# Sixteen subtractions of layer 1's weights move from the vector engine to GpSimd

## The chip, the cores and the metric

The kernel runs on one core of a Trainium2 chip. The metric is the device time of one execution in microseconds (us), as a median over runs. The core has a matrix engine (PE, also TensorE), a vector engine (DVE), a scalar engine (ACT), GpSimd (POOL) and a queue engine that issues transfers (SP). Each engine works through its own instructions strictly in the order in which the program put them, and waits on semaphores where an instruction needs another engine's result.

## The reference

The work is an attention block with a memory term, followed by two feed-forward layers; all results are float32.

```python
scores = scale * np.matmul(q, k.transpose(0, 1, 3, 2))      # B, H, S, D = 4, 8, 576, 64
...
a = np.exp(scores)
a /= a.sum(-1, keepdims=True) + 1e-09
local = np.matmul(a, v)
...
return (g * mem_out + (1 - g) * local).astype(np.float32)

h = x @ w_in                                                # 2304 x 512 by 512 x 2048
r = np.maximum(h, 0.0)
g = s * (r * r) + b
return (g @ w_out).astype(np.float32)                       # 2304 x 2048 by 2048 x 512
```

The second layer has the same two products with a leaky relu between them. The weights `w_in` and `w_out` of both layers arrive as 64-bit floats.

## The kernel before, in words

Attention is done batch by batch (b = 0 to 3) and in each batch for four pairs of heads; each pair is done in two sets of query chunks, so that a batch has eight output groups. One group goes through every engine in turn: scores on PE (L758), row maxima on DVE (L731), exponentials on ACT (L724), the sums' reciprocals on DVE (L784, L786), scaling of the weights on ACT or DVE (L543, L545), transposes on PE (L558), copies of the transposes on ACT or DVE (L566, L568), and the outputs on PE (L647, L663). L647 stands at the head of each group's outputs, so its groups count how far attention is.

The feed-forward layers work on blocks of tokens. Block 0 of layer 1 has the first 512 tokens, which are ready when batch 0 of attention is done. For each of 16 slices f of the hidden width, PE does the first product in four steps of three matmuls (L906, L907, L908 into `hb`) and the second product in four steps of three (L947, L948, L949 into `yb`). Such a step of three matmuls is called a step below. Three matmuls are needed because every float32 operand is split into a high part, rounded to the PE's faster float32 format, and a low part, which is the rest: high by high, high by low, low by high.

Block 0 also prepares layer 1's weights, slice by slice, first `w_in` (x = 0, key `wi`) and then `w_out` (x = 1, key `wo`). A 512 KB piece is loaded; DVE puts a float32 together out of the two 32-bit words in three instructions (L845, L848, L851); ACT rounds it to the high part (L854); DVE subtracts the high part from the float32 and so writes the low part (L857). All are 128 partitions by 512 columns. The float32 sits in one of a few shared buffers (`room`, `pool`, `poolx`) that is free again after the subtraction. Layer 2's weights go the same way much later.

Nothing of the order is written by hand. All operations are handed to a planner with an engine and an assumed duration each. It goes through time, gives every engine the ready operation of highest rank, hands out the shared buffers as they come free, and the instructions are then put out in that order. Attention of batches 0 and 1 ranks ahead of the weights, these ahead of batches 2 and 3, and these ahead of the feed-forward matmuls, which therefore fill what attention leaves of PE. A duration that is changed for one operation can change the order of all engines behind it.

Of the kernel before, what the change touches and what calls it, by code (L numbers as in the profile page):

```python
# [78 lines left out]
class Plan:  # L79
# [17 lines left out]
    def op(self, eng, dur, fn, r=(), w=(), prio=None, bytes_=0, claim=()):  # L97
        i = len(self.ops)
        deps, late = set(), set()
        for k in r:  # L100
            if k in self.writer:
                deps.add(self.writer[k])
            self.readers.setdefault(k, []).append(i)
        for k in w:
            if k in self.writer:
                deps.add(self.writer[k])
            late.update(self.readers.get(k, ()))
            self.writer[k] = i
            self.readers[k] = []
        late -= deps  # L110
        late.discard(i)
        deps.discard(i)
        slots = []
        for k in list(r) + list(w):
            s = k[0] if isinstance(k, tuple) else k
            if isinstance(s, Slot) and s not in slots:
                slots.append(s)
                s.left += 1
        self.ops.append((eng, dur, fn, deps | late, i + self.lean if prio is None else prio, bytes_, slots, late, claim))
        return i  # L120
# [181 lines left out]
def t_dve(n, rate=1.04, extra=0.0):  # L302
    return 69 + n * rate + extra


def t_act(n, fixed=93.0, extra=0.0):
    return fixed + n * 0.834 + extra


def build(tc, kp, vd, qp, mzd, beta8, sb2, win1, wout1, win2, wout2, alpha, outT):  # L310
    nc = tc.nc
    win1, wout1, win2, wout2 = (w.bitcast(I32) for w in (win1, wout1, win2, wout2))
    V, A, T = nc.vector, nc.scalar, nc.tensor
    plan = Plan(NSLOT, 3 * XF)
    plan.edge = NSLOT - XS
    op = plan.op
    ATT, MOE, LATE = 0, 10 ** 7, 400

    with tc.tile_pool(name="sb", bufs=1) as sb, tc.tile_pool(
# [9 lines left out]
        def wt(f, x, lo):  # L329
            if f not in made:  # L330
                made[f] = sb.tile([128, 4, DM], F32R, name=f"wt{f}", tag=f"wt{f}")
            return made[f][:, 2 * x + lo, :]
# [43 lines left out]
        def at(s, n, dt=F32):  # L376

            if s.place < NSLOT:
                t, j = (pool, s.place) if s.place < NSLOT - XS else (poolx, s.place - NSLOT + XS)
                v = t[:, j * GW:(j + s.size) * GW]  # L380
            else:
                f, j = divmod(s.place - NSLOT, 3)
                v = room[KF - XF + f][:, j * GW:(j + s.size) * GW]
            return (v if dt == F32 else v.bitcast(dt))[:, 0:n]
# [50 lines left out]
        def either(kind, a_dur, a_fn, d_dur, d_fn, **kw):  # L435

            ways = {"ACT": (a_dur, a_fn)}
            if kind in FLEX:
                ways["DVE"] = (d_dur, d_fn)
            plan.either(ways, **kw)  # L440
# [375 lines left out]
        def weights(win, wout, f, layer):  # L816
            prio = None
            if layer == 1:
                prio = marks[int(WP)] + (WP - int(WP)) * (marks[1] - marks[0])
            claim = []  # L820
            if layer == 1 and f >= KF - XF:
                claim = [NSLOT + 3 * (f - KF + XF) + j for j in range(3)]
            above = max(0, 3 * (f + 1 - KF + XF))
            for src, x, key in ((win, 0, "wi"), (wout, 1, "wo")):
                sw = Slot(RES["wb" if layer == 1 else "wb2"], layer == 1, above=above)

                def whole(sw=sw, dt=F32):
                    return at(sw, 512, dt)

                st = Slot(RES["st" if layer == 1 else "st2"], layer == 1, 2, above)  # L830

                def word(x, st=st):
                    return at(st, 1024, I32).rearrange("p (n t) -> p n t", t=2)[:, :, x]

                gate = []

                first = layer == 2 and f == x == 0
                if layer == 2:
                    gate = [("x1", B - 1, NP - 1)] if first else ["claimed"]
                elif W1GATE:  # L840
                    gate = [("x1", 0, min(NP - 1, f // W1GATE))]
                op("SP", 475, lambda st=st, src=src: nc.sync.dma_start(
                    out=at(st, 1024, I32), in_=src[f]), r=gate, w=[st] + (["claimed"] if first else []), prio=prio, bytes_=524288,
                   claim=list(range(NSLOT - XS, NSLOT)) if first else [])
                op("DVE", t_dve(512, 0.52), lambda word=word, whole=whole: V.tensor_scalar(  # L845
                    out=whole(dt=I32), in0=word(1), scalar1=3, scalar2=0x3FFFFFF8, op0=ALU.logical_shift_left,
                    op1=ALU.bitwise_and), r=[st], w=[sw], prio=prio)
                op("DVE", t_dve(512), lambda word=word, whole=whole: V.scalar_tensor_tensor(  # L848
                    out=whole(dt=I32), in0=word(0), scalar=29, in1=whole(dt=I32), op0=ALU.logical_shift_right,
                    op1=ALU.bitwise_or), r=[st], w=[sw], prio=prio)  # L850
                op("DVE", t_dve(512), lambda word=word, whole=whole: V.scalar_tensor_tensor(  # L851
                    out=whole(dt=I32), in0=word(1), scalar=-0x40000000, in1=whole(dt=I32), op0=ALU.bitwise_and,
                    op1=ALU.bitwise_or), r=[st], w=[sw], prio=prio)
                either("w", t_act(512), lambda whole=whole, x=x: A.copy(out=wt(f, x, 0), in_=whole()),  # L854
                       t_dve(512, 0.52), lambda whole=whole, x=x: V.tensor_copy(out=wt(f, x, 0), in_=whole()),
                       r=[sw], w=[(key, "h", f)], prio=prio, claim=claim)
                op("DVE", t_dve(512), lambda whole=whole, x=x: V.tensor_tensor(  # L857
                    out=wt(f, x, 1), in0=whole(), in1=wt(f, x, 0).bitcast(F32), op=ALU.subtract),
                   r=[sw, (key, "h", f)], w=[(key, "l", f)], prio=prio)

# [169 lines left out]
        def moe(layer, blk, xs):  # L1030
            t0, n = BLOCKS[layer][blk]
            if (layer, blk) != (1, 0):
                load_x(layer, blk, t0, n, xs)
            for f in range(KF):
                if layer == 1 and blk == 0:
                    weights(win1, wout1, f, 1)
                if f == 0 and (layer, blk) == (1, 1):
                    flush()
                    op("ACT", 400, ones, r=["one", ("g2", KF - 1)],
                       w=["gr"] + [(x, j) for x in ("gt", "gh", "gl") for j in range(2)])  # L1040

                if layer == 1 and n == NBIG and pend[0] is not None:
                    flush()
                gj = g1(layer, n, xs, f)
                if pend[0] is not None:
                    flush()
                pend[0] = (layer, blk, f, gj)

        def flush():
            layer, blk, f, gj = pend[0]  # L1050
            pend[0] = None
            t0, n = BLOCKS[layer][blk]
            g2(layer, blk, n, f, gj)
            if layer == 1 and blk == len(BLOCKS[1]) - 1:
                weights(win2, wout2, f, 2)
            if f == KF - 1:
                evac(layer, blk, t0, n)
# [68 lines left out]
```

## Time and profile before

| | before |
|---|---|
| median of 3 runs | 1002.53 us (1000.65 to 1002.85) |
| the profiled execution's own time | 1002.58 us |
| its span in the profile | 1000.6 us |
| PE busy | 988.0 us (99%) |
| DVE busy | 584.4 us (58%) |
| ACT busy | 461.5 us (46%) |
| POOL busy | 5.1 us (1%) |

The span runs from the first to the last instruction; 2 us of the execution's own time lie around it. The busy shares are averages over a program with very different stretches, so a share says little about any one of them.

### The profile page before, as it was taken

How to read it: one execution, taken by the hardware profiler on the slowest of the kernel's cores; microseconds unless marked ns; L12 is line 12 of the kernel's file. 1: busy time of each engine (PE TensorE's matmuls, PEld its weight loads, DVE VectorE, ACT ScalarE, POOL GpSimd, SP SyncE). 2: the span in 40 equal slices, each digit the busy share in tenths (PEclk: the TensorE clock that was granted, in tenths of full speed). 3: DMA queues.
4: the chain of work that ended last, by engine and by line, in shares of the span. 5: the costliest groups of instructions: out<-in, count | busy, mean ns of one | idle time of the engine just before them, and what ended most of it. 6: DMA issues, size and time to landing. Idle time of an engine off the chain costs nothing.

```text
span 1000.6 us, 17782 instructions
## 1 busy us (share of the span) xinstructions
PE 988.0 (99%) x7032; PEld 846.0 (85%) x7032; DVE 584.4 (58%) x1422; ACT 461.5 (46%) x1160; POOL 5.1 (1%) x29
## 2 busy tenths in 40 slices
PE   7999999999999999999999999999999999999998
PEld 5677777888899888899999998888888888888898
DVE  7999998465555765534121999945334433533354
ACT  7867776576666876654454753312111111210111
POOL 1000000000000000000000000000000000000000
PEclk9999999999999999999999999999999999999999
DMA  4446434134455545444000665502000200100010
GB/s 160 150 146 230 158 129 146 45 91 107 110 124 105 139 91 103 104 119 141 1 22 1 199 187 162 158 1 85 0 1 1 74 1 1 42 1 1 1 43 22
DMA packets 86146, 85.07 MB, mean 85 GB/s; under 512 B 56880, under 2 KB 65072, under 8 KB 86064
## 3 DMA queue, kind: packets, MB, share of 16 engines
q1 hardware_dynamic: 86064, 83.95, 29.7%
q8 instruction: 55, 0.90, 0.4%
q14 instruction: 27, 0.22, 0.1%
HBM read 57.72 MB, written 13.11 MB: 71 GB/s over the span
## 4 chain that ended last, share of the span: by engine, by line
PE 93%; DVE 3%; ACT 2%; issue 1%; DMA 0%; SPq 0%; DVEq 0%; ACTq 0%
PE yb L947 14%; PE yb L949 14%; PE yb L948 13%; PE hb L906 9%; PE hb L908 8%; PE hb L907 8%; PE sp L908 3%; PE sp L907 3%; PE sp L906 3%; PE sp L758 2%; PE ob L907 2%; PE ob L906 2%; PE ob L908 2%; PE sp L663 2%; PE ob L758 1%; PE yb L758 1%
## 5 line engine op out<-in xcount | busy, mean ns | idle before, releaser
L947 PE MATMUL yb<-gr,wt 128*128 128x256 f32 (+2 forms) x832 | 273.5, 329 | 0.1
L949 PE MATMUL yb<-gr,wt 128*128 128x256 f32 (+2 forms) x832 | 271.4, 326 | 0.6 <-DVE gr L929 0.6
L948 PE MATMUL yb<-gr,wt 128*128 128x256 f32 (+2 forms) x832 | 270.0, 324 | 0.0
L906 PE MATMUL hb<-xr,wt 128*128 128x256 f32 (+1 forms) x592 | 184.7, 312 | 0.5 <-ACT gt L920 0.5
L929 DVE TENSOR_TENSOR gr<-gt,gr 128x256 fp32r<-128x256 f32 (+1 forms) x168 | 84.0, 500 | 169.9 <-ACT gr L928 169.7
L908 PE MATMUL hb<-xr,wt 128*128 128x256 f32 (+1 forms) x592 | 180.0, 304 | 0.0
L907 PE MATMUL hb<-xr,wt 128*128 128x256 f32 (+1 forms) x592 | 179.9, 304 | 0.0
L947 PEld LDWEIGHTS yb<-gr,wt 128*128 128x128 f32 x832 | 157.0, 189 | 16.7 <-issue 1.5
L949 PEld LDWEIGHTS yb<-gr,wt 128*128 128x128 f32 x832 | 156.8, 188 | 15.8 <-DVE gr L929 1.5
L948 PEld LDWEIGHTS yb<-gr,wt 128*128 128x128 f32 x832 | 156.9, 189 | 13.5
L928 ACT CAST gr<-gt 128x256 fp32r<-128x256 f32 (+1 forms) x168 | 78.6, 468 | 148.3 <-DVE gt L926 139.5
L906 PEld LDWEIGHTS hb<-xr,wt 128*128 128x128 f32 x592 | 111.7, 189 | 12.7 <-issue 5.5
L908 PEld LDWEIGHTS hb<-xr,wt 128*128 128x128 f32 x592 | 111.6, 189 | 5.7
L907 PEld LDWEIGHTS hb<-xr,wt 128*128 128x128 f32 x592 | 111.8, 189 | 4.5
L920 ACT ACTIVATE gt<-hb 128x256 f32<-128x256 f32 (+1 forms) x128 | 52.5, 410 | 118.9 <-PE hb L908 117.9
L928 ACT CAST gr<-mz 128x512 fp32r<-128x512 f32 (+1 forms) x40 | 23.1, 578 | 158.2 <-DVE mz L926 158.1
L908 PE MATMUL sp<-xr,wt 128*128 128x512 f32 (+1 forms) x160 | 59.4, 371 | 0.0
L907 PE MATMUL sp<-xr,wt 128*128 128x512 f32 (+1 forms) x160 | 59.3, 371 | 0.0
L906 PE MATMUL sp<-xr,wt 128*128 128x512 f32 (+1 forms) x160 | 59.2, 370 | 0.0
L921 ACT ACTIVATE gt<-gt 128x256 f32<-128x256 f32 (+1 forms) x128 | 57.0, 446 | 2.7
L929 DVE TENSOR_TENSOR gr<-mz,gr 128x512 fp32r<-128x512 f32 (+1 forms) x40 | 25.5, 638 | 25.0 <-ACT gr L928 25.0
L923 DVE TENSOR_SCALAR mz<-ob,alv 128x512 f32<-128x512 f32 (+1 forms) x20 | 13.9, 697 | 40.0 <-PE ob L908 40.0
(358 smaller groups left out, 1483.8 us busy)
## 6 DMA issues: line engine op xcount, KB each, us to landing
pool<-wout SPq DMA_DIRECT2D x20, 512.0 KB, 4.4
pool<-win SPq DMA_DIRECT2D x18, 512.0 KB, 4.2
room<-win SPq DMA_DIRECT2D x11, 512.0 KB, 3.9
pool<-y SPq DMA_DIRECT2D x18, 256.0 KB, 3.6
room<-wout SPq DMA_DIRECT2D x8, 512.0 KB, 4.2
out_t<-pool SPq DMA_DIRECT2D x16, 256.0 KB, 2.1
y<-pool SPq DMA_DIRECT2D x23, 128.0 KB, 1.7
x<-pool SPq DMA_DIRECT2D x10, 288.0 KB, 2.2
```

The source lines that it names most:

```text
L663: T.matmul(obk[D * odd:D * odd + D, AT[c] - o0:AT[c] - o0 + nq], W[:, kb, odd, w], p_t(k)[:, y:y + nq], start=False, stop=False, skip_grou ...
L758: T.matmul(bank_at(bk)[rows, x:x + n], half(sqp, odd, q0, nq), half(sk, odd, k0, n), start=True, stop=True, skip_group_check=True)
L906: T.matmul(H_, W_h, X_h, start=(d == 0), stop=False)
L907: T.matmul(H_, W_h, X_l, start=False, stop=False)
L908: T.matmul(H_, W_l, X_h, start=False, stop=(d == KD - 1))
L920: op("ACT", t_act(n, 50), lambda: A.activation(out=t_, in_=H_, func=AF.Relu), r=[hk, "gr"], w=[tk], prio=-1)
L921: op("ACT", t_act(n), lambda: A.activation(out=t_, in_=t_, func=AF.Square), w=[tk], prio=-1)
L928: op("ACT", t_act(n), lambda: A.copy(out=G_h, in_=t_), r=[tk], w=[("gh", gj)], prio=-1)
L929: op("DVE", t_dve(n), lambda: V.tensor_tensor(out=G_l, in0=t_, in1=G_h.bitcast(F32), op=ALU.subtract), r=[tk, ("gh", gj)], w=[("gl", gj)], ...
L947: T.matmul(Y, W_h, G_h, start=first, stop=False, skip_group_check=True)
L948: T.matmul(Y, W_l, G_h, start=False, stop=False, skip_group_check=True)
L949: T.matmul(Y, W_h, G_l, start=False, stop=False, skip_group_check=True)
```

## The change

For layer 1 and x = 0 the subtraction of the low part goes to GpSimd, with an assumed duration of 1100 ns; for x = 1, and for all of layer 2, it stays on the vector engine. Sixteen instructions change their engine. A line is added, so that every line behind L857 has a number higher by one in the changed kernel (L857 is L858 there, L906 is L907, L947 is L948).

```diff
-                op("DVE", t_dve(512), lambda whole=whole, x=x: V.tensor_tensor(
+                low = "DVE" if layer == 2 or x == 1 else "POOL"
+                op(low, 1100.0 if low == "POOL" else t_dve(512), lambda whole=whole, x=x, e=nc.gpsimd if low == "POOL" else V: e.tensor_tensor(
                     out=wt(f, x, 1), in0=whole(), in1=wt(f, x, 0).bitcast(F32), op=ALU.subtract),
                    r=[sw, (key, "h", f)], w=[(key, "l", f)], prio=prio)
```

GpSimd's queue held 26 rows and now holds 43. This piece of the difference is the middle of its queue; `wt_464` is slice 0, `wt_653` slice 1, `wt_780` slice 2, `wt_840` slice 3, and the L549 rows clear the padding of attention weights ahead of PE's transposes.

```order
 L549 MEMSET poolx 128x64
+L858 TENSOR_TENSOR wt_464<-poolx,wt_464 128x512
 L549 MEMSET room_67 128x64
-L549 MEMSET pool 128x64 x2
-L549 MEMSET poolx 128x64 x2
+L858 TENSOR_TENSOR wt_653<-room_69,wt_653 128x512
+L858 TENSOR_TENSOR wt_780<-room_70,wt_780 128x512
+L549 MEMSET pool 128x64
+L858 TENSOR_TENSOR wt_840<-room_70,wt_840 128x512
```

The subtractions now stand in one queue with the clears, and a clear behind a subtraction waits for it.

On the vector engine the order is the same up to the first subtraction that is gone, and nearly so up to the second. Behind that it differs. These rows of before stand between the 11th and the 12th L784 of the vector engine's queue:

```order
L851 SCALAR_TENSOR_TENSOR room_69<-room_68,room_69 128x512
L848 SCALAR_TENSOR_TENSOR room_70<-poolx,room_70 128x512
L845 TENSOR_SCALAR room_68<-room_70 128x512
L568 COPY poolx<-sp_99 128x384
L857 TENSOR_TENSOR wt_1041<-room_69,wt_1041 128x512
L851 SCALAR_TENSOR_TENSOR room_70<-poolx,room_70 128x512
L848 SCALAR_TENSOR_TENSOR room_68<-room_70,room_68 128x512
L845 TENSOR_SCALAR room_69<-pool 128x512
L857 TENSOR_TENSOR wt_1128<-room_70,wt_1128 128x512
```

and these stand there in the changed kernel:

```order
L851 SCALAR_TENSOR_TENSOR room_70<-room_67,room_70 128x512
L568 COPY pool<-sp_100 128x384
L848 SCALAR_TENSOR_TENSOR room_69<-room_68,room_69 128x512
L845 TENSOR_SCALAR room_68<-room_70 128x512
L851 SCALAR_TENSOR_TENSOR room_69<-room_68,room_69 128x512
L848 SCALAR_TENSOR_TENSOR room_68<-room_70,room_68 128x512
L845 TENSOR_SCALAR room_70<-room_69 128x512
L731 ISA sp_99,mx<-sp_99,mask 128x288
```

The assembling of the weights is as dense as before, and attention's rows come sooner because the subtractions between them are fewer.

On PE the order is the same up to the middle of the first steps of block 0. Behind that, attention of batch 1 stands earlier. These rows of before lead up to the 11th group of L647 (`hb` and `yb` are the banks of the two products, `wt_916` and `wt_842` weights of two slices):

```order
L558 MATMUL sp_99<-ident,poolx 128x128 x3
L558 MATMUL sp_100<-ident,pool 128x128 x3
L906 MATMUL hb<-xr,wt_916 128x512
L907 MATMUL hb<-xr,wt_916 128x512
L908 MATMUL hb<-xr,wt_916 128x512
L947 MATMUL yb_94<-gr,wt_842 128x512
L948 MATMUL yb_94<-gr,wt_842 128x512
L949 MATMUL yb_94<-gr,wt_842 128x512
L647 MATMUL ob<-ident,pool 128x128 x2
```

and these in the changed kernel:

```order
L558 MATMUL ob<-ident,poolx 128x128 x3
L907 MATMUL hb<-xr,wt_840 128x512
L908 MATMUL hb<-xr,wt_840 128x512
L909 MATMUL hb<-xr,wt_840 128x512
L758 MATMUL sp_99<-pool,poolx 64x288 x2
L758 MATMUL sp_100<-pool,poolx 64x288 x2
L647 MATMUL ob<-ident,poolx 128x128 x2
```

Fewer steps of block 0 stand ahead of the same attention group: 33 ahead of the 11th group of L647 before and 24 now, 42 and 36 (first and second product) ahead of the 14th before and 31 and 24 now. From the 17th group (batch 2) on, the number of steps ahead of each group is the same in both.

## Rows read from the trace of the kernel before

**Rows 1.** The page: an engine's busy time; the chain that ended last, by engine

```profile
PE 988.0 (99%) x7032; PEld 846.0 (85%) x7032; DVE 584.4 (58%) x1422; ACT 461.5 (46%) x1160; POOL 5.1 (1%) x29
PE 93%; DVE 3%; ACT 2%; issue 1%; DMA 0%; SPq 0%; DVEq 0%; ACTq 0%
```

**Rows 2.** Busy time by stretch: stretch, length, engines (instructions), PEclk, DMA share, GB/s

```profile
50.00:75.00 25.00, 22.96 (x212) 17.58 (x212) 23.71 (x76) 17.02 (x52) 0.15 (x1) 0.93 0.46 145
75.00:100.00 25.00, 25.00 (x160) 19.36 (x158) 24.49 (x63) 17.77 (x42) 0.24 (x2) 1.00 0.69 230
100.00:150.00 50.00, 50.00 (x308) 37.84 (x308) 49.05 (x125) 36.03 (x88) 0.00 (x0) 1.00 0.44 144
58.00:60.00 2.00, 2.00 (x10) 1.64 (x9) 1.98 (x5) 2.00 (x7) 0.00 (x0) 0.60 0.72 287
60.00:62.00 2.00, 2.00 (x10) 1.72 (x9) 1.38 (x2) 1.05 (x4) 0.00 (x0) 0.55 0.04 12
81.40:148.30 66.90, 66.90 (x429) 51.03 (x428) 65.44 (x167) 47.68 (x112) 0.24 (x2) 1.00 0.51 167
87.50:154.80 67.30, 67.30 (x431) 51.42 (x430) 65.47 (x168) 46.95 (x110) 0.24 (x2) 1.00 0.47 151
```

**Rows 3.** Layer 1's subtractions on the vector engine: nanoseconds (min/median/max), first and last start

```profile
L857 DVE TENSOR_TENSOR wt<-room,wt x28: 658/686/693, 47.3 to 160.1; 128x512 fp32r<-128x512 f32 x28
```

**Rows 4.** The longest of PE's waits between 20 and 175 us: total, times, longest

```profile
PE sp L758 <- DVE xr L688: 0.9, 1, 0.9
```

**Rows 5.** Timeline, vector engine: start, length, line, output and inputs

```profile
39.99 0.69 DVE L857 TENSOR_TENSOR wt<-poolx,wt 128x512 fp32r<-128x512 f32 x1
...
52.85 0.69 DVE L848 SCALAR_TENSOR_TENSOR room<-pool,room 128x512 int32<-128x512 int32 x1
...
54.83 0.42 DVE L845 TENSOR_SCALAR room<-pool 128x512 int32<-128x512 int32 x1
55.17 0.16 DVE L780 TENSOR_TENSOR sm<-sm 128x1 f32<-128x1 f32 x1
...
58.15 0.69 DVE L857 TENSOR_TENSOR wt<-room,wt 128x512 fp32r<-128x512 f32 x1
58.75 0.69 DVE L851 SCALAR_TENSOR_TENSOR room<-pool,room 128x512 int32<-128x512 int32 x1
...
119.30 0.42 DVE L568 COPY pool<-sp 128x256 f32<-128x256 f32 x1
```

**Rows 6.** Timeline, PE

```profile
76.53 0.39 PE L908 MATMUL hb<-xr,wt 128*128 128x512 f32 x1
...
78.85 0.39 PE L947 MATMUL yb<-gr,wt 128*128 128x512 f32 x1
...
79.55 0.40 PE L947 MATMUL yb<-gr,wt 128*128 128x512 f32 x1
...
83.08 0.48 PE L906 MATMUL hb<-xr,wt 128*128 128x512 f32 x1
83.39 0.40 PE L907 MATMUL hb<-xr,wt 128*128 128x512 f32 x1
...
120.44 0.58 PE L647 MATMUL ob<-ident,pool 128*128 128x128 f32 x3
```

**Rows 7.** Timeline, GpSimd

```profile
0.80 0.58 POOL L390 MEMSET mask<- 128x576 bf16 x1 [0.29 <-POOLq L1119]
1.45 0.29 POOL L392 TENSOR_SCALAR_AFFINE_SELECT mask<-mask 128x128 bf16<-128x128 bf16 x1
1.69 0.34 POOL L396 MEMSET mask<- 128x288 bf16 x1
2.08 0.50 POOL L398 COPY mask<-mask 64x64 bf16<-64x64 bf16 x2
...
52.87 0.15 POOL L549 MEMSET pool<- 128x64 f32 x1 [8.48 <-PE yb L663]
```

## The prediction, made before the changed kernel was run

> **What bounds the kernel now.** I read the page first. PE is busy for 988.0 us, and the chain that ended last is 93% PE [rows 1]. So the kernel is worth what PE's order and PE's gaps are worth, and a microsecond taken from another engine shows only where PE was waiting for it. The average for the vector engine, 58%, hides the place that matters. I then read busy time by stretch [rows 2]. From 75 to 150 us, PE is busy without a gap, and the vector engine is busy for 73.5 of 75 us beside it. That is the stretch in which layer 1's weights are prepared: its 32 subtractions begin at 40 us and end at 172 us (28 of them are in one row [rows 3]). So two engines are full at once, and PE's order there is a weave of attention (which needs the vector engine at every turn) and steps of block 0 (which fill the rest).
>
> PE's gaps lie just ahead of it. From 50 to 75 us PE is idle for 2.04 us [rows 2]; the longest single wait, 0.9 us, is for a vector instruction [rows 4]. At 58 to 62 us PE's granted clock is 0.60 and 0.55, near the lower level of 1.2 GHz, after PE had stood still several times; against full clock this loses 2 x 0.40 + 2 x 0.45 = 1.7 us [rows 2]. All that a lighter vector engine can give back is therefore about 2.0 + 1.7 = 3.7 us. The rest of PE's idle time, at the start and the end and past 400 us, has no layer-1 subtraction near it.
>
> **The change, part by part.** *Removed.* Sixteen subtractions leave the vector engine. One occupies it for 0.60 us (58.15 to the next start at 58.75 [rows 5]), together 9.6 us. Only two of them stand ahead of 68 us, where PE has gaps: slice 0 at 39.99 and slice 1 at 58.15 [rows 5]. The vector engine has no spare time there, so what follows can start up to 1.2 us sooner, and PE's 2.0 us of gaps can shrink by that at most; ACT and PE's own slow clock stand behind some of them too, so I take 1.0 us gained, with 0 and 3.7 as the ends.
>
> *Moved: the order.* Behind 68 us the planner uses the lighter vector engine to bring attention of batch 1 forward. Between the 10th and the 14th group of L647, PE had 60 steps of block 0 and has 37 now. A step is 0.70 us (78.85 to 79.55 [rows 6]), so of the 67.3 us that PE needed there [rows 2], 23 x 0.70 = 16.1 go, and 51.2 us remain. The 16.1 us are not saved: the steps stand later, and PE has to do them all the same. Along the vector engine's queue I counted the same stretch from the 10th to the 14th L784, which ran from 81.4 to 148.3 us with 65.4 us busy [rows 2]. There are 20 subtractions before and 7 now, 18 and 15 of L845, 18 and 15 of L848, 19 and 16 of L851, 8 and 5 of L929 (the low part of block 0's activations), and one copy less. An L845 occupies 0.34 us (54.83 to 55.17 [rows 5]); the others are of the same shape as a subtraction, 0.60 us. Gone are 13 x 0.60 + 3 x 0.34 + 9 x 0.60 + about 0.4 = 14.6 us, and 50.8 us remain. **So the vector engine, at 50.8 us, is again as full as PE, at 51.2 us.** The planner has spent what was freed. PE's order now has 37 steps for filling where it had 60, and nothing left over if the vector engine falls behind by more than 0.4 us.
>
> How soon PE notices is seen at one copy: it ends at 119.30 + 0.42 = 119.72 us, and the outputs that need it start on PE at 120.44 us [rows 5, 6]. That is 0.7 us of slack. PE's order is fixed, so it can't take a later step in the meantime.
>
> *Added: the subtraction on GpSimd.* No row shows it. The clear of 576 columns, which reads nothing, gives 0.58 / 576 x 512 = 0.52 us as the floor; the two copies of 64 columns in 0.50 us give 0.25 x 8 = 2.0 us as the ceiling; the select of 128 columns, which reads one input, starts 0.24 us ahead of the next instruction, 0.96 us for 512 columns [rows 7]. A subtraction reads two inputs, so I take 1.1 us. The Trainium skill (GPSIMD Engine Reference, section 3.1) states 4497 ns for an addition of 2048 columns; a quarter of it is an estimate of 1.12 us, which no run here shows yet.
>
> Its length by itself does no harm. Slice 1's low part was finished at 58.84 us and first read by PE at 76.53 us [rows 5, 6], some 17 us of cover, which a microsecond of GpSimd doesn't use up. If that cover were gone, each microsecond would be PE's. Five clears now stand behind subtractions in GpSimd's queue, and nine L845 wait for GpSimd, to get the buffer that a subtraction held; these have less cover, and I put 0 to 0.5 us on each.
>
> *Added: two engines in the same memory at once.* This is the open price. Of the 50.8 us, 43 instructions (L848, L851, L857, L929) read two tensors from SBUF at 0.60 us, and two L497 do so; 15 L845 and 8 L545 run at about twice the usual rate per column. That is about 27 + 5 + 2 = 34 us, 68% of the vector engine's time. If GpSimd's reading holds such an instruction up, a subtraction of 1.1 us costs the vector engine 0.68 x 1.1 = 0.75 us, more than the 0.60 us that it took there. The trace bounds it loosely. A GpSimd clear at 52.87 us ran beside an L848 at 52.85 us, which took its usual 0.69 us [rows 5, 7]: no hold. But a clear only writes, so it says nothing about two readers. The ends are 0 and 1.1 us per subtraction; I take 0.75, since the freed time can be kept only if GpSimd's two reads and the vector engine's two go on side by side, which nothing here has shown. About seven GpSimd subtractions fall into the stretch (as many as the `w_out` ones): 7 x 0.75 = 5.2 us. The vector engine then needs 56.0 us against PE's 51.2, and PE waits 4.8 us; with 0.6 us of it caught in existing slack, 4.2 us. Past the 14th group the vector engine was busy less (it had ended its weights by 172 us), and I add nothing.
>
> The Trainium skill (SBUF — State Buffer, section "Who interferes with whom") says that a vector instruction with two SBUF inputs contends with a GpSimd instruction that reads SBUF and not with one that only writes, and that the later one stands still until the first has finished. The clear beside the L848 agrees with the second half, with 0.69 us; no row of before shows the first. By that section of the Trainium skill the sum is the one below; without a hold it would be that of the first rival.
>
> *Smaller.* A float32r step right behind an attention matmul costs PE 0.31 us for its first matmul in place of 0.70 / 3 = 0.23 [rows 6]. The changed order has 160 changes between the two kinds, before 166: 6 x 0.08 = 0.5 us gained.
>
> **The sum.** 1002.58 (own time of the profiled execution, 0.05 above the median of the runs) - 1.0 - 0.5 + 4.2 = 1005.3 us, and 1005.2 against the median.
>
> **The rivals.** *GpSimd and the vector engine don't hold each other up* (the other side). For it: the clear beside the L848. Then the plan works as ordered, 1002.6 - 1.0 - 0.5 = 1001.1 us, and 999.4 us if the shorter gap ahead of 58 us also keeps PE's clock up. It decides at a hold of under (51.2 - 50.8 + 1.5) / 7, about 0.3 us per subtraction. *GpSimd is the one that waits*: it gets in only when the vector engine has a stretch of PSUM work (the L731 rows). The weights' 17 us of cover hide that, the nine buffer waits may cost some: 1001 to 1003 us. *The dear subtraction*: at the copy's rate of 2.0 us a hold is 0.68 x 2.0 = 1.36 us, seven make 9.5 us, and clears and buffers come late as well: 1002.6 - 1.5 + 9.5 - 1.0 = 1009.6 us or more. *Nothing is seen*, because PE is the bound: it is, but its order was rewoven, so I give this no case of its own.
>
> **How the numbers follow.** I give the forecast 0.45, no hold 0.30, GpSimd waiting 0.15, the dear subtraction 0.10. A measurement of this kernel can tell about 0.2%, that is 2 us: faster means below 1000.5, slower above 1004.5. Slower: 0.38 of the forecast's 0.45 and all of the 0.10, 0.48. Faster: half of no hold, 0.15, and 0.05 of the others, 0.20. The same: 0.32. The forecast's own range is 1003.5 to 1008; the range over the cases runs from 999.5 (no hold with the clock kept) to 1009.5 (the dear subtraction).
>
> **What would show it.** In the profile of the changed kernel: 16 GpSimd subtractions of about 1.1 us; L848, L851 and L857 beside them longer than 0.69 us, or late starts between them (right), or none of it (first rival); GpSimd's subtractions themselves stretched (second rival). PE waiting between 75 and 150 us, where it waited nowhere before, by about 4 us in total, released by the vector engine; the gaps of 50 to 75 us smaller by about 1 us; the 14th group of L647 near 142 us rather than 154.8. I am wrong if PE shows no waits there, or if they are released by GpSimd's low parts themselves.

## The result: 0.7% slower

The changed kernel takes 1008.71 us (median of 6 runs, 1007.87 to 1011.70), the kernel before 1002.18 us beside it (median of 6, 1000.65 to 1002.85). The ratio over all runs is 1.0073, with a 95% interval of 1.0057 to 1.0089; between the medians the difference is 6.5 us. That is well beyond the 0.2% that can be told from no change. The time lies inside the range over the predicted cases (999.5 to 1009.5), but above the forecast's own range (1003.5 to 1008). The profiled execution took 1010.75 us (span 1009.0) at a mean clock of 0.996; another one at 0.997 took 1011.70, and the four at 0.999 or 1.0 took 1007.87 to 1008.79.

The page of the changed kernel, against [rows 1]: busy time by engine, and the chain that ended last.

```profile
PE 992.0 (98%) x7032; PEld 846.2 (84%) x7032; DVE 584.0 (58%) x1402; ACT 463.6 (46%) x1164; POOL 28.6 (3%) x45
PE 88%; DVE 7%; ACT 3%; issue 1%; DMA 0%; SPq 0%; DVEq 0%; ACTq 0%
```

The vector engine has 20 instructions fewer and is as busy as before (584.0 us, before 584.4), although sixteen subtractions have left it. In the chain its share rose from 3 to 7%, at PE's cost. Busy time by stretch, against [rows 2]:

```profile
50.00:75.00 25.00, 22.23 (x203) 17.40 (x203) 22.15 (x69) 17.60 (x52) 2.92 (x3) 0.86 0.35 115
75.00:100.00 25.00, 24.32 (x152) 17.13 (x151) 24.35 (x63) 18.75 (x49) 4.46 (x3) 1.00 0.62 206
100.00:150.00 50.00, 47.17 (x329) 34.28 (x328) 49.72 (x118) 32.89 (x79) 11.13 (x10) 1.00 0.53 174
58.00:60.00 2.00, 1.80 (x6) 1.18 (x6) 1.64 (x5) 2.00 (x7) 0.00 (x0) 0.54 0.96 260
60.00:62.00 2.00, 2.00 (x11) 1.80 (x10) 1.26 (x5) 1.36 (x5) 0.00 (x0) 0.50 0.68 272
62.00:66.00 4.00, 3.54 (x23) 2.91 (x23) 3.04 (x11) 2.87 (x11) 0.00 (x0) 0.63 0.00 0
```

PE, which had no gap from 75 to 150 us, is idle there for 0.68 + 2.83 = 3.5 us. From 100 to 150 us the vector engine is busy for 49.72 us with 118 instructions, where it did 125 in 49.05 us: fewer instructions, more time. The subtractions, by line and engine (nanoseconds: min/median/max, first and last start), and PE's waits from 20 to 175 us (total, times, longest), against [rows 3, 4]:

```profile
L858 DVE TENSOR_TENSOR wt<-room,wt x15: 649/682/998, 47.1 to 163.3; 128x512 fp32r<-128x512 f32 x15
L858 POOL TENSOR_TENSOR wt<-room,wt x13: 1289/1406/1961, 55.7 to 158.4; 128x512 fp32r<-128x512 f32 x13
```

```profile
PE sp L513 <- ACT pool L724: 1.3, 1, 1.3
PE sp L758 <- DVE xr L688: 1.1, 1, 1.1
PE sp L758 <- ACT pool L724: 0.8, 1, 0.8
PE sp L470 <- DVE pool L568: 0.8, 1, 0.8
```

About half of PE's waiting is released by ACT's exponentials (L724), whose input is the vector engine's row maxima. To see what held that engine, two timelines are read side by side (start, length, line). GpSimd's first:

```profile
55.75 1.38 POOL L858 TENSOR_TENSOR wt<-room,wt 128x512 fp32r<-128x512 f32 x1 [11.34 <-ACT wt L854]
...
108.12 1.33 POOL L858 TENSOR_TENSOR wt<-room,wt 128x512 fp32r<-128x512 f32 x1 [4.99 <-ACT wt L854]
115.74 1.96 POOL L858 TENSOR_TENSOR wt<-room,wt 128x512 fp32r<-128x512 f32 x1 [6.29 <-ACT wt L854]
```

and the vector engine's:

```profile
56.31 0.83 DVE L784 SCALAR_TENSOR_TENSOR sm<-sm,wsc 128x5 f32<-128x5 f32 x1
57.07 0.42 DVE L731 CUSTOM_DVE_ANT_0 sp<-sp,mask 128x256 f32<-128x256 f32 x1
...
108.22 1.25 DVE L780 TENSOR_TENSOR sm<-sm 128x1 f32<-128x1 f32 x1
...
115.53 0.42 DVE L845 TENSOR_SCALAR room<-room 128x512 int32<-128x512 int32 x1
115.86 0.69 DVE L851 SCALAR_TENSOR_TENSOR room<-room,room 128x512 int32<-128x512 int32 x1
116.47 0.43 DVE L731 CUSTOM_DVE_ANT_0 ob<-ob,mask 128x256 f32<-128x256 f32 x1
...
117.19 1.05 DVE L848 SCALAR_TENSOR_TENSOR room<-room 128x512 int32<-128x512 int32 x1
```

The same L784 in the kernel before:

```profile
56.29 0.15 DVE L784 SCALAR_TENSOR_TENSOR sm<-sm,wsc 128x5 f32<-128x5 f32 x1
```

This L784 of five columns, 0.15 us long there, begins at 56.31 us in the changed kernel and ends at 57.14, when GpSimd's subtraction ends (55.75 + 1.38 = 57.13). An L780 of a single column takes 1.25 us and ends at 109.47, GpSimd at 109.45. At 115.74 it goes both ways: GpSimd's subtraction runs into an L845 and the L851 at 115.86, which keep their 0.42 and 0.69 us, while the subtraction takes 1.96 us in place of 1.29; the L848 at 117.19 is then held until GpSimd is done. The L731 between the L851 and the L848, with one input in PSUM, keeps its length. Against the median of the same form and line in the kernel before, 12 vector instructions between 30 and 180 us are too long by more than 0.05 us, by 9.9 us together (the **held time** below). The 16 subtractions that left had taken 16 x 0.60 = 9.6 us. GpSimd's own sixteen sum to 23.7 us, 3.1 more than 16 x 1.29.

Where the time went is seen at four marks on PE: the first `hb` matmul of block 0, and the 10th, 14th and 17th group of L647 (from the 17th on both kernels have the same steps ahead of each group). Of the kernel before, from the first `hb` matmul and from the 14th to the 17th group (the stretch between is in [rows 2]):

```profile
67.83:87.46 19.63, 19.63 (x116) 14.72 (x114) 19.59 (x50) 13.88 (x31) 0.00 (x0) 1.00 0.81 275
...
154.81:221.69 66.88, 66.83 (x450) 53.32 (x449) 41.61 (x123) 42.11 (x111) 0.35 (x2) 1.00 0.34 97
```

and of the changed kernel, all three:

```profile
69.76:91.35 21.59, 21.59 (x129) 15.49 (x127) 21.11 (x53) 16.34 (x39) 4.56 (x5) 1.00 0.72 242
91.35:147.31 55.96, 52.45 (x351) 37.51 (x350) 55.27 (x135) 36.69 (x91) 12.20 (x10) 1.00 0.52 174
147.31:230.00 82.69, 82.64 (x519) 65.84 (x518) 49.58 (x135) 50.67 (x125) 4.84 (x5) 1.00 0.28 85
```

The first `hb` matmul is 69.76 - 67.83 = 1.9 us late. From there to the 17th group, a stretch that I call the **weave**, PE needs 153.9 us before and 160.2 after, 6.4 us more. At the 17th group the changed kernel is 8.3 us behind, and it stays there: 775.3 us are left to PE's last matmul before (997.0 - 221.7) and 775.4 after. Of the 6.4 us only 3.5 show as idle time, in a weave with 991 matmuls before and after. PE's rows overlap (three matmuls of 0.39 us in 0.70 us [rows 6]), so a wait that is shorter than the overlap shows as a busy PE.

### The profile page after: what moved, and what is told of

Read it like the earlier page. It is cut to its first block, busy times and chain, and to the rows that moved or that the text cites. A ratio compares the mean times of both kernels' runs of the same rounds, so it can differ in the third digit from the quotient of the medians.

```text
span 1009.0 us, 17814 instructions
## 1 busy us (share of the span) xinstructions
PE 992.0 (98%) x7032; PEld 846.2 (84%) x7032; DVE 584.0 (58%) x1402; ACT 463.6 (46%) x1164; POOL 28.6 (3%) x45
## 4 chain that ended last, share of the span: by engine, by line
PE 88%; DVE 7%; ACT 3%; issue 1%; DMA 0%; SPq 0%; DVEq 0%; ACTq 0%
PE yb L948 13%; PE yb L950 13%; PE yb L949 13%; PE hb L907 8%; PE hb L908 8%; PE hb L909 8%; PE sp L909 3%; PE sp L908 3%; PE sp L907 3%; PE sp L758 2%; PE ob L908 2%; PE ob L907 2%; PE ob L909 2%; PE yb L758 1%; PE sp L663 1%
## 5 line engine op out<-in xcount | busy, mean ns | idle before, releaser
L948 PE MATMUL yb<-gr,wt 128*128 128x256 f32 (+2 forms) x832 | 273.3, 328 | 0.1
L930 DVE TENSOR_TENSOR gr<-gt,gr 128x256 fp32r<-128x256 f32 (+1 forms) x168 | 84.7, 504 | 179.2 <-ACT gr L929 179.0
L907 PE MATMUL hb<-xr,wt 128*128 128x256 f32 (+1 forms) x592 | 184.6, 312 | 0.5 <-ACT gt L921 0.5
L948 PEld LDWEIGHTS yb<-gr,wt 128*128 128x128 f32 x832 | 157.0, 189 | 16.0 <-issue 0.8
L907 PEld LDWEIGHTS hb<-xr,wt 128*128 128x128 f32 x592 | 111.9, 189 | 10.9 <-issue 4.1
L907 PE MATMUL sp<-xr,wt 128*128 128x512 f32 (+1 forms) x160 | 59.2, 370 | 0.0
L930 DVE TENSOR_TENSOR gr<-mz,gr 128x512 fp32r<-128x512 f32 (+1 forms) x40 | 25.5, 638 | 25.3 <-ACT gr L929 25.3
```

The lines of the kernel that those rows point to most:

```text
L907: T.matmul(H_, W_h, X_h, start=(d == 0), stop=False)
L930: op("DVE", t_dve(n), lambda: V.tensor_tensor(out=G_l, in0=t_, in1=G_h.bitcast(F32), op=ALU.subtract), r=[tk, ("gh", gj)], w=[("gl", gj)], ...
L948: T.matmul(Y, W_h, G_h, start=first, stop=False, skip_group_check=True)
```

## The experiments

Three theories first. **Hold theory**: GpSimd's reading holds vector instructions with two SBUF inputs (or at the doubled rate), and PE waits for these. **Order theory**: the new order of PE's steps costs time by itself. **Lateness theory**: low parts and clears come late out of GpSimd's queue. The held time and the weave of each profiled execution stand in this table with the times; "before" was run beside each group of kernels (1001.58 us beside runs 1 to 4, 1001.73 beside 5 to 8, 1001.39 beside 9 to 11 and 1001.69 beside 12; 14 to 17 runs each). The ratios are taken over all runs and can differ a little from the quotient of the medians.

| kernel | median us (runs) | ratio to before, 95% interval | held us | weave us |
|---|---|---|---|---|
| before | 1002.18 (6) | | | 153.9 |
| changed | 1008.71 (6) | 1.0073 [1.0057, 1.0089] | 9.9 | 160.2 |
| 1 before's order, on GpSimd | 1006.65 (6) | 1.0040 [1.0025, 1.0054] | 7.0 | 155.2 |
| 2 changed order, on the vector engine | 1008.05 (5) | 1.0066 [1.0054, 1.0078] | 0 | 159.4 |
| 3 changed order, GpSimd only clears | 1001.94 (11) | 1.0003 [0.9994, 1.0012] | 0.8 | 154.6 |
| 4 before, GpSimd reads besides | 1004.74 (5) | 1.0030 [1.0018, 1.0042] | 5.8 | 157.6 |
| 5 planner told of the hold | 1004.83 (6) | 1.0033 [1.0020, 1.0045] | 9.2 | 156.4 |
| 6 slices 0 and 1 stay | 1010.48 (4) | 1.0085 [1.0072, 1.0098] | 9.0 | 163.0 |
| 7 slices 0 and 1 only | 1003.85 (11) | 1.0018 [1.0009, 1.0027] | 0.7 | 154.1 |
| 8 four pieces | 1006.63 (5) | 1.0047 [1.0035, 1.0059] | 5.1 | 157.9 |
| 9 order of 6, GpSimd only clears | 1004.13 (10) | 1.0025 [1.0016, 1.0034] | 1.3 | 155.7 |
| 10 order of 6, on the vector engine | 1008.40 (5) | 1.0072 [1.0060, 1.0085] | 0 | 160.7 |
| 11 layer 2 in place of layer 1 | 1006.66 (5) | 1.0057 [1.0044, 1.0071] | 12.5 (layer 2) | 153.9 |
| 12 changed order, GpSimd copies | 1003.32 (11) | 1.0015 [1.0006, 1.0024] | 3.2 | 155.1 |

**1. Before's order, subtractions on GpSimd.**

```diff
+                low = nc.gpsimd if layer == 1 and x == 0 else V
-                op("DVE", t_dve(512), lambda whole=whole, x=x: V.tensor_tensor(
+                op("DVE", t_dve(512), lambda whole=whole, x=x, e=low: e.tensor_tensor(
```

> The order of before on every engine (it is still planned with the vector engine), but the sixteen subtractions are issued on GpSimd at their old places. Hold theory (GpSimd's reads and the vector engine's two-input or doubled-rate instructions keep each other waiting): the vector engine gets back 16 x 0.60 = 9.6 us and loses about 10 us again in holds, at other places than before; 1001.5 to 1005 us, with instructions held for 0.3 to 1.1 us visible. Order theory (only the rewoven order costs): 1000.5 to 1002.2 us, never slower than before. Lateness theory (GpSimd's 1.3 us and the buffers it frees late): within 1 us of before.

**2. The changed kernel's order, subtractions on the vector engine.**

```diff
-... e=nc.gpsimd if low == "POOL" else V: e.tensor_tensor(
+... e=V: e.tensor_tensor(
```

> The order of the changed kernel on every engine, but the sixteen subtractions are issued on the vector engine at the places where the plan had them on GpSimd. No hold is possible, and the vector engine carries 9.6 us that its order was not planned for. Hold theory: nearly as slow as the changed kernel, 1006 to 1010 us, since about the same time is put on the vector engine in the same order. Lateness theory: about 1002 us, since nothing waits for GpSimd. Order theory: 1008 us as well, so this run speaks to lateness and to what a microsecond on the vector engine costs in this order.

**3. The changed kernel's order, GpSimd clears the low part and the buffer.**

```diff
-... e.tensor_tensor(
-                    out=wt(f, x, 1), in0=whole(), in1=wt(f, x, 0).bitcast(F32), op=ALU.subtract),
+... [nc.gpsimd.memset(t, 0.0) for t in (wt(f, x, 1).bitcast(F32), whole())] ...
```

> The order of the changed kernel, but in place of each subtraction GpSimd clears the low part and then the buffer (two writes of 128x512, no read); layer 1's first product so lacks its low weights. Timing of waits and of the buffer's release stays: the second clear waits for the scalar engine as the subtraction did. Hold theory with only reads held against two-input instructions: the vector engine is held little (by its doubled-rate L845 and L545 at most), 1000 to 1003 us. Order theory: 1007 to 1009 us as the changed kernel. Lateness theory: 1005 to 1008 us if the two clears take about 1.1 us together.

**4. The kernel before, GpSimd subtracts the high part from itself into a spare tile, beside the real subtraction.**

```diff
+                        h = wt(f, x, 0).bitcast(F32)
+                        for c in (0, 256):
+                            nc.gpsimd.tensor_tensor(out=idle, in0=h[:, c:c + 256], in1=h[:, c:c + 256], op=ALU.subtract)
...
```

> The kernel before, all sixteen subtractions still on the vector engine, and beside each of them GpSimd subtracts the high part from itself into a scratch tile (two instructions of 256 columns, nobody reads the result). Order and work of all other engines are those of before. Hold theory: the vector engine is held for 0.4 to 0.7 us by each pair, 6 to 11 us in all, with nothing given back: 1006 to 1013 us. Order theory and lateness theory: 1002 us, as before.

Run 3 decides. It has the changed kernel's order, and its clears come out of the same queue, but GpSimd reads nothing; the loss is gone (1001.94 us). So neither the order nor the queue costs the 6.5 us. (Its two clears together are shorter than a subtraction and free the buffer sooner; but the changed kernel's vector engine is idle for only 55.96 - 55.27 = 0.7 us between the 10th and the 14th group, so it hardly waits for late buffers.) Its busy time by stretch:

```profile
66.45:87.90 21.45, 21.45 (x129) 15.58 (x126) 20.44 (x53) 16.50 (x39) 3.22 (x8) 1.00 0.70 243
87.90:138.40 50.50, 49.98 (x352) 37.18 (x351) 49.05 (x135) 36.70 (x91) 8.91 (x18) 1.00 0.56 193
138.40:221.10 82.70, 82.66 (x520) 65.85 (x519) 48.59 (x135) 50.72 (x125) 2.93 (x7) 1.00 0.29 85
```

Row by row against the changed kernel: 21.45 and 21.59 us, 82.70 and 82.69 us, but 50.50 and 55.96 us from the 10th to the 14th group. The hold costs PE 5.5 us there (3.0 of it as idle time) and nothing on either side, and the vector engine's busy time falls from 55.27 to 49.05 us with the same 135 instructions. Run 2 costs what the change costs, with no hold at all and nothing on GpSimd that could come late, so the Lateness theory's 1002 us falls: the order was planned for a vector engine lighter by 9.6 us, and it hardly matters whether these come back as subtractions or as holds (weaves of 159.4 and 160.2 us). Run 4 shows the hold without any change of order: reading that is of no use to anybody costs 0.30%. It costs less than I had expected of the Hold theory (1004.74 us against 1006 to 1013, and 5.8 us held against 6 to 11), and the 1002 us of the other two theories is missed on the other side. One reason may be that the vector engine once kept GpSimd out: four instructions, two pairs of 1.30 us when undisturbed, took 10.89 us, 8.48 of them the second one. From 121.5 to 128.9 us the vector engine had two-input and doubled-rate instructions one behind another, and none of them was held:

```profile
120.26 10.89 POOL L862 TENSOR_TENSOR idle<-wt 128x256 bf16<-128x256 f32 x4 [3.73 <-ACT wt L855]
```

Run 1's median, 1006.65 us, lies above what I had expected of the Hold theory (1001.5 to 1005). Two executions at full clock took 1002.94 and 1003.68 us, inside that range; four at 0.994 to 0.998 took 1006.0 to 1007.5. So most of its 0.40% goes with PE's clock and not with waits that the holds make directly. Its profile is of a full-clock one, and its weave is only 1.3 us longer: with 60 steps of block 0 for filling, most of the 7.0 us of holds seem to fall where PE has other work.

**5. The planner is told: 900 ns on the vector engine beside each GpSimd subtraction.**

```diff
+                if low == "POOL":
+                    op("DVE", 900.0, lambda: None, r=[(key, "h", f)], prio=prio)
```

> The changed kernel, but its planner is also told of 900 ns on the vector engine for each subtraction that GpSimd does (no instruction is put out for them); so attention of batch 1 is brought forward less: between the 10th and the 14th group of L647 PE's order has 46 steps of block 0, where the changed kernel has 37 and the kernel before 60. Hold theory (a reading GpSimd holds the vector engine by about 0.6 us per subtraction, and that costs PE only where the order has no slack): vector instructions are still held by 7 to 10 us, but PE's waits in 75 to 150 us fall from 3.5 to under 1.5 us; 1003.5 us (1001.5 to 1005.5). Rival, Fixed-price theory (each such subtraction costs PE about 0.4 us wherever it stands, whatever the order): 1008 us (1006.5 to 1010).

**6 and 7. The first two slices stay on the vector engine; only the first two go.**

```diff
-                low = "DVE" if layer == 2 or x == 1 else "POOL"
+                low = "DVE" if layer == 2 or x == 1 or f < 2 else "POOL"
```

(run 6; run 7 has `f >= 2` in its place)

> The changed kernel with the subtractions of slices 0 and 1 left on the vector engine; 14 go to GpSimd, planned as in the changed kernel. Hold theory: the late start of the first hb matmul (1.9 us in the changed kernel) came from the hold under slice 1's subtraction and is gone, the first hb matmul at 68.5 us or sooner; the weave behind it loses 14/16 of its 6.4 us; 1007.0 us (1005.0 to 1008.5). Rival, Early theory (the start decides, and the gaps behind it follow from a start that came late): 1003 us (1001.5 to 1004.5).

> The mirror image: only the subtractions of slices 0 and 1 go to GpSimd, the other 14 stay on the vector engine. Hold theory: two holds of up to 1 us ahead of 70 us, the first hb matmul up to 1.9 us late, and behind it a weave with slack that loses nothing: 1002.5 us (1001.3 to 1004.5). Early theory: the start is late and the loss grows behind it: 1006 to 1008 us.

Run 5 supports the Hold theory: 9.2 us are held, nearly as much as in the changed kernel, but the weave grows by 2.5 us in place of 6.4, and PE is idle for 0.7 us between 75 and 150 us:

```profile
75.00:150.00 75.00, 74.27 (x501) 56.45 (x498) 70.37 (x171) 53.85 (x130) 14.58 (x12) 1.00 0.50 163
```

There is no fixed price per subtraction then; what a held microsecond costs depends on the work that PE's order has ready. Run 7 lies in the Hold theory's range, and its weave is as long as before's. Its one profile, of an execution of 1002.29 us, doesn't show where its median gets 2 us from, but the clocks do in part: six executions at 0.999 took 1002.29 to 1003.89 us, five at 0.997 or 0.998 took 1003.85 to 1005.09. At full clock its first `hb` matmul comes at 67.18 us, though the L784 at 55.98 is held as in the changed kernel; in run 2, where no subtraction is on GpSimd, it comes at 67.19, and in run 3, without reading, at 66.45. So, from one profile each, the hold at 56 us eats the 0.7 us that a lighter vector engine would give there. Run 6 was a miss: 1010.48 us, above what either theory expected. Runs 9 and 10 were made to find out why.

**8. Each GpSimd subtraction cut into four of 128 columns.**

```diff
+... [nc.gpsimd.tensor_tensor(
+                    out=wt(f, x, 1)[:, c:c + 128], in0=whole()[:, c:c + 128], in1=wt(f, x, 0).bitcast(F32)[:, c:c + 128], op=ALU.subtract)
+                    for c in range(0, 512, 128)] ...
```

> The changed kernel's order, with each GpSimd subtraction cut into four of 128 columns. Hold theory in its plain form (what counts is how long GpSimd reads while the vector engine has two-input work): as much or more is held in sum, in more and shorter pieces of 0.2 to 0.5 us, 10 to 16 us in all; 1009.5 us (1007.5 to 1013). Rival, Length theory (a single hold of 1 to 1.8 us harms because it is longer than the 0.7 us of slack that copies have; short ones are swallowed): 1004.5 us (1002 to 1006.5).

A miss for the sum that I expected of the Hold theory, and the Length theory's time is missed by a hair too. GpSimd took far longer (64 pieces, 40.5 us in place of 23.7), and yet the vector engine was held for 5.1 us, half as much. The vector engine's rows say how:

```profile
101.78 0.94 DVE L851 SCALAR_TENSOR_TENSOR room<-room,room 128x512 int32<-128x512 int32 x1
102.65 0.94 DVE L848 SCALAR_TENSOR_TENSOR room<-room,room 128x512 int32<-128x512 int32 x1
```

beside GpSimd's:

```profile
101.06 2.84 POOL L858 TENSOR_TENSOR wt<-room,wt 128x128 fp32r<-128x128 f32 x4 [7.51 <-ACT wt L854]
```

Each of these vector instructions waits for part of one piece, 0.26 us (0.94 in place of 0.68); no single hold exceeds 0.27 us, where the changed kernel's reach 1.2. The four pieces, which take 1.7 us undisturbed (slice 0's), needed 2.84: in between GpSimd waited for the vector engine. Here the two take turns by whole instructions, so the length of GpSimd's instruction bounds what the vector engine loses at a time. They don't always: in run 4 GpSimd got no turn for some 8 us.

**9 and 10. The order of run 6, with GpSimd clearing (as run 3), and with all subtractions on the vector engine (as run 2).**

> The order of the kernel whose first two subtractions stay, but GpSimd clears the low part and the buffer in place of the other 14 subtractions (two writes, no reads; the first product lacks the low part of 14 slices of weights). Hold theory: its whole loss of 8.7 us is holds, so it is at 1002 us (1001 to 1003.5), as the changed kernel with clears was. Tight-order theory (this order has so little slack that PE waits in it anyhow): 1004 to 1007 us.

> The same order with all 16 subtractions done by the vector engine where the 14 stood for GpSimd: no holds, but 14 x 0.6 = 8.4 us put back. In the changed kernel's order the same edit lost 6.3 us. Hold theory: the loss goes by the microseconds that the vector engine has too many, 1007.5 us (1005.5 to 1009.5). Rival, Place theory (holds cost more than their length, since they come at one instruction that others wait for, in lumps of 1 us): clearly below its sister with GpSimd, 1005 us (1003 to 1006.5).

Run 6 loses 8.75 us, run 9 still 2.74 us, each against its own runs of before: 6.0 us go with the reading, and 2.7 stay without it, with 1.3 us of holds. So the Hold theory alone, with its 1001 to 1003.5 us, fails for this order. Run 9's time lies just inside the Tight-order theory's range, but the waits that this theory speaks of don't show: PE waits for 0.2 us between 68 and 175 us, in a weave that is 1.8 us longer than before's. What costs the 2.7 us stays open. Run 10 lies in the Hold theory's range and above the Place theory's. It loses 7.0 us, though, and its sister with GpSimd 8.75, so a smaller extra price of the place isn't excluded.

**11. Layer 1 as before; layer 2's first-product subtractions go to GpSimd.**

```diff
+                low = "DVE" if layer == 1 or x == 1 else "POOL"
```

> Layer 1 as in the kernel before; the 16 first-product subtractions of layer 2 go to GpSimd instead, in the stretch from about 550 to 660 us, where PE is at 49.5 to 50.0 of 50 us and the vector engine at 47 of 50. Hold theory: vector instructions are held by some 6 to 10 us there too, but PE's filling work there is long and the weights are ahead of their use, so little is lost: 1002.5 us (1001 to 1004.5). Fixed-price theory (0.4 us of PE per subtraction): 1008 us.

Slower by 5.3 us: above the Hold theory's range and 1.3 us short of the Fixed-price theory's 1008. My cover was wrong: PE's filling work needs the vector engine itself. PE's largest sum of waits between 540 and 660 us (total, times, longest); the kernel before waited there for 0.5 us in all, at L906:

```profile
PE yb L950 <- DVE gr L930: 3.7, 4, 1.3
```

One of its causes on the vector engine, the subtraction on GpSimd beside it:

```profile
566.31 1.50 DVE L930 TENSOR_TENSOR gr<-gt,gr 128x256 fp32r<-128x256 f32 x1
```

```profile
566.06 1.47 POOL L858 TENSOR_TENSOR wt<-pool,wt 128x512 fp32r<-128x512 f32 x1 [3.76 <-ACT wt L854]
```

and PE behind them:

```profile
567.87 0.39 PE L950 MATMUL yb<-gr,wt 128*128 128x256 f32 x1 [0.63 <-DVE gr L930]
```

The L930 that writes the low part of a block's activations lasts from 566.31 to 567.81 us, 1.08 us too long, and the second product's third matmul waits for it. Here most of a lump of 1 us reaches PE, 0.63 us of it as idle time, as that matmul is next in PE's order.

**12. The changed kernel's order, GpSimd copies in place of subtracting (the first product gets the unsplit weight as its low part).**

```diff
-... e.tensor_tensor(
-                    out=wt(f, x, 1), in0=whole(), in1=wt(f, x, 0).bitcast(F32), op=ALU.subtract),
+... nc.gpsimd.tensor_copy(out=wt(f, x, 1), in_=whole()) ...
```

> The changed kernel's order, but GpSimd copies the buffer into the low part in place of subtracting (one read and one write in place of two reads and one write; the first product gets the unsplit weight where its low part belongs). Two-readers theory (what holds the vector engine is a GpSimd instruction with two inputs): held sum under 2 us, 1002.5 us (1001.3 to 1004). Any-read theory (a GpSimd instruction that reads at all holds it for as long as it runs): each hold up to the copy's length; if a copy takes 0.7 to 1.0 us against the subtraction's 1.29, 5 to 8 us are held in all, and 1005.5 us (1004 to 1008).

Between the two. The time is in the Two-readers theory's range, but 3.2 us were held, where it said under 2: one read is enough to hold. The Any-read theory's 5 to 8 us weren't reached, as a copy that isn't held takes only 0.62 us, half of a subtraction. (A copy doesn't need ACT's high part, so it also starts sooner: it waits for the vector engine's L851.) One of the ten held instructions, 0.83 us in place of 0.69 on the vector engine, and the copy on GpSimd that ran ahead of it:

```profile
97.54 0.83 DVE L848 SCALAR_TENSOR_TENSOR room<-room,room 128x512 int32<-128x512 int32 x1
```

```profile
97.22 0.62 POOL L858 CAST wt<-room 128x512 fp32r<-128x512 f32 x1 [9.32 <-DVE room L851]
```

The four kernels with the changed order on GpSimd line up by held time: 0.8, 3.2, 5.1 and 9.9 us held, weaves of 154.6, 155.1, 157.9 and 160.2 us.

No kernel here beats the kernel before. The best, run 3, does less work than the reference asks for and only equals it.

## Why the prediction was right, and where its terms were off

*The mechanism was right.* The forecast said that two full engines have no room for a hold, that GpSimd's reads would hold the vector engine by more than was freed, and that PE would wait between 75 and 150 us, where it had waited nowhere. PE's 3.5 visible idle microseconds there answer to "about 4"; the releasers are mostly ACT, one step behind the vector engine, not the vector engine alone as I wrote. Low parts release none of the waits, so the cover of 17 us was enough. The 14th group came at 147.3 us, not near 142.

*The size was low, and the range helped.* Against the kernel before, the forecast was +2.7 us, and +6.5 were measured, close to the +7.0 of the dear subtraction. That the time lies inside the stated range is in part luck: the upper end was put at 1009.5 us for a subtraction of 2.0 us with late clears and buffers, and that isn't what happened.

*The hold, +4.2 us, was somewhat small.* I took 0.75 us for each of seven subtractions, 5.2 us, and a stretch of 51.2 us plus 4.2. Between the 10th and the 14th group, eight subtractions reach in, and 7.2 us were held, 0.90 us each; over all sixteen it is 9.9 / 16 = 0.62. A subtraction takes 1.29 us undisturbed, where I took 1.1. PE's stretch came out at 55.96 us, the forecast's was 55.4; against run 3's 50.50 the hold is worth 5.5 us. (The 34 of 50.8 us behind the 0.75 are 67%, not 68%, which changes nothing.)

*The step that failed was the gain of 1.0 us ahead of 68 us.* In the profiled execution it came out as a loss of 1.9. I costed the two freed subtractions there and not the hold of the one at 55.75 us, which catches the L784 ahead of the row maxima; these go to ACT's exponentials, for which PE's scores wait. PE on both sides of this wait, in the changed kernel:

```profile
56.45 0.91 PE L758 MATMUL sp<-poolx,pool 64*128 64x384 f32 x2 [1.05 <-DVE xr L688]
58.20 2.07 PE L758 MATMUL sp<-poolx,pool 64*128 64x384 f32 x6 [0.84 <-ACT pool L724]
```

and the second of these rows in run 7:

```profile
57.87 1.13 PE L758 MATMUL sp<-poolx,pool 64*128 64x384 f32 x6 [0.83 <-ACT pool L724]
```

In the profiled execution of the changed kernel the clock then stayed at or near its lower level, 1.2 GHz, until 65 us; over 58 to 66 us that is 2 x 0.46 + 2 x 0.50 + 4 x 0.37 = 3.4 us lost against full clock, where before lost 1.7 us [rows 2]. That difference, 1.7 us, is most of the 1.9. Run 7 has the same hold at full clock, and its six scores take 1.13 us in place of 2.07. Its first `hb` matmul, at 67.18 us, is 0.4 us later than in run 11 (66.81), whose layer 1 is that of before and whose clock was full there. So at full clock this term is a loss of some 0.4 us and still no gain, and the clock is part of why the profiled execution lies 2.0 us above the median. Whether the hold makes the low clock likelier no run tested by itself. The counts speak for it: a mean clock below 0.998 stands beside 13 of the 50 executions of the kernels in which GpSimd reads ahead of 70 us (the changed one and runs 1, 4, 5, 7, 8 and 12), and beside 1 of 103 of the others. That is no proof of a cause.

*The smaller gain of 0.5 us wasn't seen.* Run 3, without reads, has a weave 0.8 us longer than before, with 0.8 us of holds on L845 and 0.5 us of PE idle in the middle stretch. I had also missed that 12 L758 matmuls go from the middle stretch to the one ahead of the 10th group; this is why that grew from 19.63 to 21.45 us in run 3 and the middle one could need 50.5 us. It is work moved, and costs nothing.

The sum by terms, for the profiled execution: forecast -1.0 - 0.5 + 4.2 = +2.7; measured +1.9 (start), +0.8 (order, in run 3's weave) and +5.6 (160.2 - 154.6, hold) = +8.3 us, its distance at the 17th group. With 0.4 for the start at full clock it is +6.8, near the 6.5 between the medians.

*The rivals.* No hold: run 3 is what it would have been, and it gives 1001.94 us against 1001.58, not 1001.1 or 999.4. Even a GpSimd that only writes gains nothing here; PE had no gap behind 75 us to fill. GpSimd waits: it does, by 3.1 us in sum, unnoticed. The dear subtraction: 1.29 to 1.96 us is nearer to my 1.1 than to 2.0, but its hold of 0.9 us per subtraction in the dense stretch lies between that case's 1.36 and my 0.75; its late clears and buffers don't show.

The Trainium skill (SBUF — State Buffer, section "Who interferes with whom") says that the later of two such instructions stands still until the first is done. The rows at 55.75 and 56.31 us agree (L784 ends with GpSimd). At 115.74 us GpSimd came while an L845 ran and stood still, which agrees too; but the L851 that started 0.12 us after GpSimd's row went ahead of it, which that sentence alone doesn't give. It also says that a GpSimd instruction that only writes doesn't contend with two SBUF inputs; run 3 agrees, since its 0.8 us are all on L845, which has one input at the doubled rate.

## What to carry to other kernels

Work that is moved to an idle engine is only off the busy one if the two don't hold each other up, as GpSimd and the vector engine did here: count the hold, by what share of the busy engine's instructions can be held and how long the guest's instruction is, and set it against what was freed. Here 9.6 us were freed and 9.9 us held. Keep the guest's instructions short where it must be, let it write or copy rather than read two tensors, and tell the planner what the hold costs (run 5 lost 3.1 us in place of 6.5); and ask first whether the engine that sets the time has a gap at all that the freed time could fill.

## What the runs showed of the hardware that was not expected

An instruction of one column waits as long as one of 512: an L780 of 128x1 took 1.25 us behind a GpSimd subtraction, 0.16 us before [rows 5].

The hold is two-sided: vector instructions lost up to 1.2 us behind 512 GpSimd columns and 0.26 us behind 128, and GpSimd once stood for some 8 us behind a vector engine with two-input and doubled-rate instructions back to back (run 4).

A GpSimd copy of 512 columns takes 0.62 us alone, a clear 0.53, a subtraction 1.29.
